# Linear attention and a bilinear feed-forward on one core: a column a chunk for the outputs' scale, the keys' features a slot later, the parts of v spread, and two kinds of hi parts written by ScalarE instead of GpSimd

## The chip, the cores and the metric

The kernel runs on one core of one Trainium2 chip. The metric is the device time of one execution in microseconds (us). Engines are named as in the profile: PE is TensorE (PEld its weight loads), DVE is VectorE, ACT is ScalarE, POOL is GpSimd, SP is SyncE, whose queue issues most of the transfers here.

## What is computed

The reference is a kernelised attention (8 batches, 8 heads, 576 positions, head size 64, 128 features) and then a feed-forward on 4608 tokens of width 512:

```python
def phi(x):
    proj = np.einsum('bhsd,md->bhsm', x, omega)
    sq = np.sum(x * x, axis=-1, keepdims=True) / 2.0
    h = proj - sq
    h = h - np.max(h, axis=-1, keepdims=True)
    return np.exp(h) / np.sqrt(m)
q_p, k_p = (phi(q_s), phi(k_s))
kv = np.einsum('bhsm,bhsd->bhmd', k_p, v)
z = np.sum(k_p, axis=2)
num = np.einsum('bhsm,bhmd->bhsd', q_p, kv)
den = np.einsum('bhsm,bhm->bhs', q_p, z)[..., None] + 1e-06
out = num / den
...
a = x @ w1
b = x @ w2
h = a * b @ w3
return h @ w_out
```

Everything is float32 (the weights arrive as float64), and `w3 @ w_out` is one matrix that the kernel makes first, W.

## The kernel before

**Precision.** Every float32 operand of a large product is held as two float16 parts: a hi part (the value rounded) and a lo part (value minus hi). A product is then three passes on PE: hi by hi, hi by lo, lo by hi (`PASSES`). So each operand costs a hi operation (a scaled copy) and a lo operation (a subtraction) on some engine. `split` (L135 to L148), `in_parts` (L292 to L298) and `gate` (L630 to L632) do it, and strings such as `KS`, `VS`, `EH`, `EL` say for each chunk which engine does which part: in `VS`, `a` is ACT for hi and DVE for lo, `m` is POOL for hi and DVE for lo.

**The work of a chunk.** The 4608 positions are 36 chunks of 128. For a chunk of q or k: load `qraw` or `kraw` (256 KB, SP's queue, two buffers each); sum of squares on ACT (`junk_q`, `junk_k`, L158); a scale from a small PE product and DVE operations (`norm_q_k`, L163 to L178, L232); hi on ACT (L141) and lo on DVE (L144) into `qhl` and `khl`; 24 matmuls into a pair of PSUM banks (`qpj`, `kpj`, L265); the greatest entry (`nm`, DVE, L275); the subtraction (`qe`, `ke`, DVE, L288); the exponential on ACT (L289); hi and lo parts of the features (`eq`, `ek`: casts at L130 on DVE or L132 on ACT, lo at L298, mostly POOL). The features of q are transposed by DMA (`eqT`, L368).

**Batches.** A batch of 576 positions is five chunks, some of them half. Its v is loaded (`vraw`, L309), measured, scaled and split (`vhl`, L143 or L141 and L144; zeros at L332), and `kv_batch` multiplies features of k by v (`kvp`, 120 matmuls, L346; parts `kv`, L355 and L356).

**Attention and feed-forward of a chunk.** `q_attend` (`nu`, 24 matmuls, L381) and DVE's division (`gd`, `gr`, `xs`, L390 to L396), the greatest entry and its power of two (`mx`, `p2p`, `p2r`, `pt`, L403 to L414), hi on ACT (L417) and lo on DVE (L418) into `xhl`, and a DMA transpose into `xT` (L422). Then two gate units a chunk: 48 matmuls (`ab`, L617), the first half's scaled copy on ACT (`asb`, L626), the product on DVE (L627), hi on POOL (L631), lo on POOL (L632) into a block of `arena`. `project_out` (24 matmuls, `o`, L643) multiplies by W, ACT scales the result (L647) by `osc`, a DVE operation at L639, and SP's queue stores it.

**Buffers that matter.** `qpj`, `kpj`, `nu` and `kvp` take turns in two pairs of PSUM banks: the tile after the next can be written only when this one has been read. A `nu` is read by `xs`, a `kvp` by `kv`, a `kpj` by the subtraction `ke`. `osc` is a pool tile with four buffers: the write of the fifth waits until the ACT operation at L647 has read the first.

**Order.** Python code lays the work out in slots, three for a step, and within a slot by a rank: step i brings `q_chunk(i)` (rank 1) and `k_chunk(i + 5)` (rank 2), and `q_attend` some slots later. Each slot runs one unit of a queue of gates and projections, then what is planned, then one part of v's work (`v_unit`); a batch's leftover parts are run just before its `kv_batch`. What a scheduler then makes of it is a fixed order on every engine; each engine runs its instructions strictly in that order.

Of the kernel before, what the change touches and what calls it, by code (L numbers as in the profile page):

```python
# [9 lines left out]
F32 = mybir.dt.float32  # L10
# [5 lines left out]
ALU = mybir.AluOpType  # L16
# [3 lines left out]
P = 128  # L20
# [10 lines left out]

KS = "a"
QS = "a"
VS = "aaaaam"
WS = "a"
EH = "aaaaaadadadada"
EL = "ddddddpdpdpp"
# [13 lines left out]
EAGER = 40  # L51
EARLY = 6
KV_LAG = 5
RAW64_BUFS = 3
O_BUFS = 2
RAW_BUFS = 2
# [10 lines left out]
def tile_favor_attention_then_bilinear_ffn(  # L67
# [19 lines left out]
    nc = tc.nc  # L87
    NCH = qT.shape[0]
# [14 lines left out]
    const = ctx.enter_context(tc.tile_pool(name="const", bufs=1))  # L103
# [9 lines left out]
    def bank_m(name):  # L113
        return ps_m.tile([P, 512], F32, tag="pm", name=name)

    def small(name, n=1, rows=P, dt=F32, bufs=4):
        return sm.tile([rows, n], dt, tag=f"s_{name}", name=name, bufs=bufs)
# [16 lines left out]
    def pick(kinds, i):  # L134
        return kinds[min(i, len(kinds) - 1)]  # L135
# [82 lines left out]
    for i in range(4):  # L218
        t = const.tile([P, 3], F32, name=f"sums_{i}")
# [82 lines left out]
    def k_chunk(c):  # L302
        e = features(c, "k")
        ek[c] = at.tile([P, 2, H, M], F16, tag="ek", name=f"ek_{c}", bufs=EK_BUFS)
        in_parts(ek[c], e, pick(EH, c), pick(EL, c))
# [20 lines left out]
    def v_split(b, n):  # L326
# [9 lines left out]
        x = vraw[c][r0:r1]  # L336
        split(pick(VS, 5 * b + n), hi, lo, x, sv[b][r0:r1])

# [103 lines left out]
    arena = const.tile([P, ARENA, 512], F32, name="arena")  # L442
    raw_at = list(range(0, 4 * RAW64_BUFS, 4))
    mag_at = list(range(4 * RAW64_BUFS, 4 * RAW64_BUFS + 4, 2))
    free = list(range(4 * RAW64_BUFS + 4, ARENA))

# [157 lines left out]
    def gate(c0, n, u):  # L604

        nf, T = 4 // n, n * P
        x = xT[c0 * P // TOK]
        off = c0 * P % TOK
        ab = []
        for m in range(2):  # L610
            ps = bank_m(f"ab_{c0}_{u}_{m}").rearrange("p (f s) -> p f s", f=nf)
            for k in range(nf):
                f = u * nf + k
                i, r = f // (NF // 2), f % (NF // 2)
                mm = [(cc, a, b) for cc in range(NC) for a, b in PASSES]
                for j, (cc, a, b) in enumerate(mm):
                    nc.tensor.matmul(  # L617
                        ps[:, k],
                        w12[m][i][cc][:, a, r * P : (r + 1) * P],
                        x[:, b, cc, off : off + T],  # L620
                        start=j == 0,
                        stop=j == len(mm) - 1,
                    )
            ab.append(ps)
        asb = mo.tile([P, nf, T], F32, tag="asb", name=f"asb_{c0}_{u}", bufs=ASB_BUFS)
        nc.scalar.mul(asb, ab[0], 2.0**-37)  # L626
        nc.vector.tensor_tensor(asb, ab[1], asb, ALU.mult)  # L627
        place = block()
        left[place] = nf * n
        h = arena[:, place].bitcast(F16).rearrange("p (x f s) -> p x f s", x=2, f=nf)  # L630
        nc.gpsimd.tensor_scalar(h[:, 0], asb, 1.0, 1.0, ALU.mult, ALU.mult)  # L631
        nc.gpsimd.tensor_tensor(h[:, 1], asb, h[:, 0], ALU.subtract)  # L632
        for k in range(nf):
            for t in range(n):
                hs[c0 + t, u * nf + k] = h[:, :, k, t * P : (t + 1) * P], place

    def project_out(c):
        sc = small("osc")
        nc.vector.tensor_scalar(sc, pts[c], pts[c], kap, ALU.mult, ALU.mult)  # L639
        ps = bank_m(f"o_{c}")  # L640
        mm = [(f, a, b) for f in range(NF) for a, b in PASSES]
        for i, (f, a, b) in enumerate(mm):
            nc.tensor.matmul(ps, hs[c, f][0][:, a], W[f][:, b], start=i == 0, stop=i == len(mm) - 1)  # L643
        for f in range(NF):
            used(hs[c, f][1])
        o = mo.tile([P, DO], F32, tag="o", name=f"o_{c}", bufs=O_BUFS)
        nc.scalar.mul(o, ps, sc)  # L647
        nc.sync.dma_start(out[c * P : (c + 1) * P, :], o)
# [3 lines left out]
    B_OF_K = {}  # L652
# [3 lines left out]
    v_work = []  # L656
# [7 lines left out]
    def v_unit():  # L664
        if v_work:
            v_work.pop(0)[1]()
# [26 lines left out]
    for ch in ORDER:  # L693
        n = seen.get(ch, 0)
# [23 lines left out]
    def put(slot, rank, fn):  # L718
        plan.setdefault(slot, []).append((rank, len(plan[slot]) if slot in plan else 0, fn))

    behind_by = []

    def ready(c):
        x_turn(c)
# [14 lines left out]
    def step(i):  # L739
        at0 = begin[i]  # L740
        kc = i + LEAD
        keys = [(n, c) for n, c in (("q", i), ("k", kc)) if 0 <= c < NCH]
        state = {}

        def norms():
            state["am"] = norm(keys, i)

        def splits():
            for name, c in keys:
                split_raw(c, name)  # L750
                if c + 2 < NCH:
                    load(srcs[name], c + 2, name)

        put(at0 - 3, 3, norms)
        put(at0 - 2, 6, lambda: scale(keys, state["am"]))
        put(at0 - 1, 8, splits)
        if i >= 0:
            put(at0, 1, lambda: q_chunk(i))
            lag = 2 if i < EARLY else 5
            put(at0 + lag, 7 if i < EARLY else 0, lambda: q_attend(i))  # L760
            put(at0 + lag + 1, 0, lambda: ready(i))
        if kc < NCH:
            put(at0, 2, lambda: k_chunk(kc))
        if kc in B_OF_K:

            def kv():

                while v_work and v_work[0][0] <= B_OF_K[kc]:
                    v_unit()
                kv_batch(B_OF_K[kc])  # L770


            put(at0 + (2 if i < 0 else KV_LAG - 1 if i < EARLY else KV_LAG), 5, kv)
        for b in range(B):
            cs = [c for c, _, _ in chunks_of(b)]
            if cs[1] == kc:
                put(at0, 9, lambda b=b: v_batch(b))
            if cs[0] == kc:
                put(at0 + 2, 10, lambda cs=cs: [v_load(c) for c in cs if c not in vraw])

    for i in range(first, NCH):
        step(i)
# [4 lines left out]
    for t in range(max(plan) + 1):  # L787
        n = min(PER[t] if t < len(PER) else 1, len(ticks))
        weights(n)
        if not ticks and raw_at:  # L790
            for a, w in [(a, 4) for a in raw_at] + [(a, 2) for a in mag_at]:
                free.extend(range(a, a + w))
            raw_at.clear()
        unit(RESERVE if t > EAGER else 0)
        for _, _, fn in sorted(plan.get(t, []), key=lambda x: x[:2]):
            fn()
        v_unit()
    assert not ticks
    while queue:
        unit()  # L800
# [38 lines left out]
```

## Time and profile before

| what | value |
|---|---|
| three timed runs | 904.66, 906.85, 910.05 us (median 906.85) |
| the profiled execution | 904.25 us, its span 902.5 us |
| mean granted PE clock | 0.951 |
| PE busy | 790.9 us, 88% of the span |
| DVE busy | 622.6 us, 69% |
| ACT busy | 421.0 us, 47% |
| POOL busy | 322.2 us, 36% |

In the rows below, times are us from the span's start and the mean of one instruction is in ns. "[2.68 <-DVE xs L396]" behind a row of the timeline says that its engine sat idle for 2.68 us before it and that DVE's `xs` ended the wait. In a row of groups, "busy, mean | idle" stand in that order. In the rows by stretch, the last three numbers are PE's granted clock (1 is full), the DMA share and GB/s.

### The profile page before, as it was taken

The numbers are of one execution on the slowest core, as the hardware profiler recorded it, in microseconds if no ns is written. First come the engines' busy times: TensorE is split into PE (matmuls) and PEld (weight loads), VectorE is DVE, ScalarE is ACT, GpSimd is POOL, SyncE is SP. The second block draws the span as 40 slices with busy tenths as digits, with TensorE's granted clock in tenths as the row PEclk, the third lists the DMA queues.
The fourth block names the chain that finished last, engine by engine and source line by source line (L and its number), as shares of the span: only waits on it lengthen the run. The fifth ranks groups of instructions, "written<-read, shape, count | busy, mean of one in ns | idle before, by whom it ended". The sixth has DMA issues, their size and how long they took to land.

```text
span 902.5 us, 20601 instructions
## 1 busy us (share of the span) xinstructions
PE 790.9 (88%) x8614; PEld 586.0 (65%) x8614; DVE 622.6 (69%) x1116; ACT 421.0 (47%) x748; POOL 322.2 (36%) x327
## 2 busy tenths in 40 slices
PE   1964499578996998999999999899899899999998
PEld 0433254476875876767777776777677677677674
DVE  5879877788779887766867777778667774553210
ACT  3677874877436535444354335543454333221111
POOL 0000003223364465443634643455444543323221
PEclk9985699789999999999999999999999999999999
DMA  8535455332345353333434443344332232333000
GB/s 311 191 120 196 140 153 170 111 73 55 88 107 105 84 130 83 83 84 83 116 83 77 95 111 71 72 94 113 85 93 65 60 71 61 82 60 60 24 25 35
DMA packets 142525, 88.43 MB, mean 98 GB/s; under 512 B 116704, under 2 KB 116832, under 8 KB 142432
## 3 DMA queue, kind: packets, MB, share of 16 engines
q1 hardware_dynamic: 134944, 66.15, 31.0%
q10 hardware_dynamic: 7488, 20.97, 6.9%
q8 instruction: 67, 1.10, 0.5%
q14 instruction: 26, 0.21, 0.1%
HBM read 49.35 MB, written 9.44 MB: 65 GB/s over the span
## 4 chain that ended last, share of the span: by engine, by line
PE 42%; DVE 28%; ACT 13%; DMA 9%; issue 6%; POOL 1%; SPq 0%; DVEq 0%; ACTq 0%; POOLq 0%
PE ab L617 20%; PE o L643 11%; DVE nm L275 5%; DVE qhl L144 4%; DMA qraw<-qT 4%; PE wp L557 4%; DVE vhl L144 3%; ACT ke L289 2%; DVE qe L288 2%; DVE ke L288 2%; DMA kraw<-kT 2%; ACT ek L132 2%; PE kvp L346 2%; DVE asb L627 2%; PE nu L381 1%
## 5 line engine op out<-in xcount | busy, mean ns | idle before, releaser
L617 PE MATMUL ab<-xT,w12b 128*128 128x256 f16 (+1 forms) x3840 | 400.3, 265 | 10.8 <-DMA xT<-xhl 8.5
L617 PEld LDWEIGHTS <-w12b 128*128 128x128 f16 x3840 | 345.1, 99 | 54.3 <-issue 8.8
L643 PE MATMUL o<-Wb,arena 128*128 128x512 f16 x864 | 193.4, 379 | 2.1 <-DVE Wb L144 1.6
L643 PEld LDWEIGHTS <-arena 128*128 128x128 f16 x864 | 84.3, 100 | 96.3 <-issue 2.9
L631 POOL TENSOR_SCALAR arena<-asb 128x512 f16<-128x512 f32 x72 | 57.6, 800 | 249.7 <-DVE asb L627 238.3
L298 POOL TENSOR_TENSOR eq<-qe,eq 128x1024 f16<-128x1024 f32 x34 | 73.9, 2174 | 147.9 <-DVE eq L130 111.1
L289 ACT ACTIVATE qe<-qe,ln_e,es 128x1024 f32<-128x1024 f32 x31 | 38.4, 1239 | 138.0 <-DVE qe L288 138.0
L632 POOL TENSOR_TENSOR arena<-asb,arena 128x512 f16<-128x512 f32 x72 | 91.4, 1270 | 5.9
L627 DVE TENSOR_TENSOR asb<-ab,asb 128x512 f32<-128x512 f32 x72 | 49.4, 686 | 52.7 <-PE ab L617 50.6
L144 DVE SCALAR_TENSOR_TENSOR qhl<-qraw,s,qhl 128x512 f16<-128x512 f32 x36 | 63.8, 1773 | 28.7 <-ACT qhl L141 28.7
L158 ACT ACTIVATE junk_q<-qraw 128x512 bf16<-128x512 f32 x36 | 22.7, 630 | 120.4 <-DMA qraw<-qT 120.3
L298 POOL TENSOR_TENSOR ek<-ke,ek 128x1024 f16<-128x1024 f32 x28 | 60.2, 2149 | 41.4 <-DVE ek L130 39.8
L265 PE MATMUL kpj<-om,khl 64*128 64x128 f16 x864 | 36.9, 237 | 43.4 <-DVE xs L396 12.1
L639 DVE TENSOR_SCALAR osc<-pt,kap 128x1 f32<-128x1 f32 x36 | 9.5, 271 | 84.8 <-ACT o L647 84.6
L265 PEld LDWEIGHTS <-khl 64*128 64x128 f16 x864 | 29.4, 103 | 50.2 <-ACT junk_k L158 16.1
L557 PE MATMUL wp<-w12b 128*128 128x512 f32 x128 | 60.2, 623 | 1.2 <-DVE w12b L485 1.2
L626 ACT ACTIVATE asb<-ab 128x512 f32<-128x512 f32 x72 | 41.8, 580 | 24.4 <-PE ab L617 24.4
L381 PEld LDWEIGHTS <-eqT 128*128 128x128 f16 (+1 forms) x960 | 32.5, 102 | 26.0 <-DMA eqT<-eq 15.3
L647 ACT ACTIVATE o<-o,osc 128x512 f32<-128x512 f32 x36 | 24.2, 673 | 52.2 <-PE o L643 52.2
L381 PE MATMUL nu<-kv,eqT 128*128 128x65 f16 (+1 forms) x960 | 34.7, 196 | 15.0 <-DMA eqT<-eq 14.3
L418 DVE SCALAR_TENSOR_TENSOR xhl<-xs,p2r,xhl 128x512 f16<-128x512 f32 x36 | 28.8, 800 | 26.5 <-ACT xhl L417 26.4
L143 POOL TENSOR_SCALAR vhl<-vraw,s 128x512 f16<-128x512 f32 (+1 forms) x35 | 36.3, 1054 | 29.4 <-DVE mx L409 11.7
(124 smaller groups left out, 1071.1 us busy)
## 6 DMA issues: line engine op xcount, KB each, us to landing
kraw<-kT SPq DMA_DIRECT2D x36, 256.0 KB, 3.0
vraw<-v SPq DMA_DIRECT2D x36, 256.0 KB, 3.0
qraw<-qT SPq DMA_DIRECT2D x36, 256.0 KB, 2.7
out<-o SPq DMA_DIRECT2D x36, 256.0 KB, 2.0
arena<-w3T ACTq DMA_DIRECT2D x8, 1024.0 KB, 5.9
arena<-w ACTq DMA_DIRECT2D x8, 1024.0 KB, 5.6
arena<-wo ACTq DMA_DIRECT2D x4, 1024.0 KB, 5.1
eqT<-eq SPq DMA_TRANSPOSE x72, 3.1
```

Of the source, the lines that this page charges most:

```text
L144: nc.vector.scalar_tensor_tensor(lo, src, s, hi, ALU.mult, ALU.subtract)
L265: nc.tensor.matmul(pg[:, g, i], hl[d, x, i], om[d, y], start=first is None and n == 0, stop=n == len(PASSES) - 1,)
L275: nc.vector.tensor_reduce(nm, pj, AX.X, ALU.max, negate=True)
L289: nc.scalar.activation(e, e, AF.Exp, scale=es, bias=ln_e)
L298: (nc.vector if lo == "d" else nc.gpsimd).tensor_tensor(t[:, 1], e, t[:, 0], ALU.subtract)
L381: nc.tensor.matmul(nu[r0:r1, h // 4, h % 4], t[:, x, place(h), r0:r1], kvs[b][:, y, h], start=n == 0, stop=n == 2,)
L557: nc.tensor.matmul(ps, w[:, j, k * P : (k + 1) * P], guest[:, j], start=j == j0, stop=j == HALF - 1,)
L617: nc.tensor.matmul(ps[:, k], w12[m][i][cc][:, a, r * P : (r + 1) * P], x[:, b, cc, off : off + T], start=j == 0, stop=j == len(mm) - 1,)
L627: nc.vector.tensor_tensor(asb, ab[1], asb, ALU.mult)
L631: nc.gpsimd.tensor_scalar(h[:, 0], asb, 1.0, 1.0, ALU.mult, ALU.mult)
L632: nc.gpsimd.tensor_tensor(h[:, 1], asb, h[:, 0], ALU.subtract)
L643: nc.tensor.matmul(ps, hs[c, f][0][:, a], W[f][:, b], start=i == 0, stop=i == len(mm) - 1)
```

## The change

Five edits:

- `oscs` is one constant tile with a column for each of the 36 chunks, in place of the four rotating `osc` buffers. The operation and its place in the program text stay.
- From step 8 on (`K_LATE`), `k_chunk` is planned one slot later than `q_chunk` of the same step, so another unit of the queue stands between them.
- The work on v gets a due slot, that of its batch's `kv_batch`; each slot runs as many parts of it as are needed to be done in time, at least one.
- `VS`: the hi parts of v are ACT's in all batches (before, ACT's for five parts and POOL's for the other 35).
- The hi part of a gate's output (72 of them) is a copy on ACT, no longer an operation on POOL. Its lo part stays on POOL.

```diff
-VS = "aaaaam"
+VS = "a"
...
+K_LATE = 8
...
-        nc.gpsimd.tensor_scalar(h[:, 0], asb, 1.0, 1.0, ALU.mult, ALU.mult)
+        nc.scalar.copy(h[:, 0], asb)
         nc.gpsimd.tensor_tensor(h[:, 1], asb, h[:, 0], ALU.subtract)
...
+    oscs = const.tile([P, NCH], F32, name="oscs")
+
     def project_out(c):
-        sc = small("osc")
+        sc = oscs[:, c : c + 1]
         nc.vector.tensor_scalar(sc, pts[c], pts[c], kap, ALU.mult, ALU.mult)
...
-            put(at0, 2, lambda: k_chunk(kc))
+            put(at0 + (i >= K_LATE), 2, lambda: k_chunk(kc))
...
-            put(at0 + (2 if i < 0 else KV_LAG - 1 if i < EARLY else KV_LAG), 5, kv)
+            due[B_OF_K[kc]] = at0 + (2 if i < 0 else KV_LAG - 1 if i < EARLY else KV_LAG)
+            put(due[B_OF_K[kc]], 5, kv)
...
-        v_unit()
+
+        n = max([1] + [-(-(k + 1) // max(due[b] - t, 1)) for k, (b, _) in enumerate(v_work)])
+        for _ in range(n):
+            v_unit()
```

Lines of the kernel after are one higher than before from the features on, and four higher from `project_out` on. In names, the first number is the chunk (for a gate, the first chunk of its group and the unit), the last the buffer's.

On PE, from the keys of chunk 15 on, the 24 matmuls of `kpj` move from between the two gate units of a chunk to behind the second; all else there keeps its order, but for the interleaving of the first projection `o_0` with `nu_4`. On DVE, the greatest entry and subtraction of the keys move with them. This is DVE before, from the second-last gate product of group 16 to its last:

```order
L627 TENSOR_TENSOR asb_16_2_7410<-ab_16_2_1_7385,asb_16_2_7410 128x512
L275 TENSOR_REDUCE nm_7451<-qpj_21_7426 128x8
L288 TENSOR_TENSOR qe_21_7453<-qpj_21_7426,nm_7451 128x1024
L275 TENSOR_REDUCE nm_7487<-kpj_26_7462 128x8
L288 TENSOR_TENSOR ke_26_7489<-kpj_26_7462,nm_7487 128x1024
L130 CAST eq_21_7456<-qe_21_7453 128x1024
L627 TENSOR_TENSOR asb_16_3_7554<-ab_16_3_1_7529,asb_16_3_7554 128x512
```

And the same place on DVE after the change:

```order
L628 TENSOR_TENSOR asb_16_2_7396<-ab_16_2_1_7371,asb_16_2_7396 128x512
L276 TENSOR_REDUCE nm_7437<-qpj_21_7412 128x8
L289 TENSOR_TENSOR qe_21_7439<-qpj_21_7412,nm_7437 128x1024
L131 CAST eq_21_7442<-qe_21_7439 128x1024
L628 TENSOR_TENSOR asb_16_3_7507<-ab_16_3_1_7482,asb_16_3_7507 128x512
L276 TENSOR_REDUCE nm_7537<-kpj_26_7512 128x8
L174 TENSOR_SCALAR norm_q22_k27_7545<-norm_q22_k27_7545 128x3
L289 TENSOR_TENSOR ke_26_7539<-kpj_26_7512,nm_7537 128x1024
```

The cast of q's features, which needs ACT's exponential, now follows directly on the subtraction, and the keys come behind the second gate product.

The second place is DVE from the lo part of the keys to the lo part of x, in the same chunk; before:

```order
L144 SCALAR_TENSOR_TENSOR khl_27_7640<-kraw_27_7056,s3_4_7563,khl_27_7640 128x512
L390 TENSOR_SCALAR gd_7627<-nu_20_7602 128x8
L394 RECIPROCAL gr_7629<-gd_7627 128x8
L639 TENSOR_SCALAR osc_8865<-pt_19_7420,kap_111 128x1
L396 TENSOR_TENSOR xs_20_7631<-nu_20_7602,gr_7629 128x512
L403 TENSOR_REDUCE mx_7633<-xs_20_7631 128x1
L409 TENSOR_SCALAR mx_7633<-mx_7633 128x1
L184 TENSOR_SCALAR p2p1_4_7701<-mx_7633 128x1
L187 RECIPROCAL p2r1_4_7703<-p2p1_4_7701 128x1
L414 TENSOR_SCALAR pt_20_7705<-p2p1_4_7701,pv_5784 128x1
L418 SCALAR_TENSOR_TENSOR xhl_20_7707<-xs_20_7631,p2r1_4_7703,xhl_20_7707 128x512
```

After:

```order
L145 SCALAR_TENSOR_TENSOR khl_27_7625<-kraw_27_7043,s3_4_7549,khl_27_7625 128x512
L391 TENSOR_SCALAR gd_7612<-nu_20_7587 128x8
L395 RECIPROCAL gr_7614<-gd_7612 128x8
L397 TENSOR_TENSOR xs_20_7616<-nu_20_7587,gr_7614 128x512
L404 TENSOR_REDUCE mx_7618<-xs_20_7616 128x1
L410 TENSOR_SCALAR mx_7618<-mx_7618 128x1
L185 TENSOR_SCALAR p2p1_4_7686<-mx_7618 128x1
L188 RECIPROCAL p2r1_4_7688<-p2p1_4_7686 128x1
L415 TENSOR_SCALAR pt_20_7690<-p2p1_4_7686,pv_5775 128x1
L643 TENSOR_SCALAR oscs_114<-pt_20_7690,kap_111 128x1
L419 SCALAR_TENSOR_TENSOR xhl_20_7692<-xs_20_7616,p2r1_4_7688,xhl_20_7692 128x512
```

The scale of an output stood ahead of `xs` and was that of chunk 19, for whose buffer the output of chunk 15 had to be scaled first; now it is that of chunk 20, directly behind its input `pt`.

The third place is ACT over one chunk, from the hi part of x to the scaling of an output; before:

```order
L417 ACTIVATE xhl_19_7422<-xs_19_7341,p2r1_4_7418 128x512
L626 ACTIVATE asb_16_2_7410<-ab_16_2_0_7360 128x512
L289 ACTIVATE qe_21_7453<-qe_21_7453,ln_e_82,es_7275 128x1024
L626 ACTIVATE asb_16_3_7554<-ab_16_3_0_7504 128x512
L289 ACTIVATE ke_26_7489<-ke_26_7489,ln_e_82,es_7275 128x1024
L132 CAST ek_26_7492<-ke_26_7489 128x1024
L141 ACTIVATE qhl_22_7635<-qraw_22_7051,s3_4_7563 128x512
L141 ACTIVATE khl_27_7640<-kraw_27_7056,s3_4_7563 128x512
L158 ACTIVATE junk_q24_8190,sums_0_101<-qraw_24_7638 128x512
L647 ACTIVATE o_15_7599<-o_15_7574,osc_7572 128x512
```

After:

```order
L418 ACTIVATE xhl_19_7408<-xs_19_7327,p2r1_4_7404 128x512
L627 ACTIVATE asb_16_2_7396<-ab_16_2_0_7346 128x512
L159 ACTIVATE junk_k28_7735,sums_3_107<-kraw_28_7339 128x512
L632 CAST arena_112<-asb_16_2_7396 128x512
L290 ACTIVATE qe_21_7439<-qe_21_7439,ln_e_82,es_7262 128x1024
L627 ACTIVATE asb_16_3_7507<-ab_16_3_0_7457 128x512
L632 CAST arena_112<-asb_16_3_7507 128x512
L290 ACTIVATE ke_26_7539<-ke_26_7539,ln_e_82,es_7262 128x1024
L142 ACTIVATE qhl_22_7620<-qraw_22_7038,s3_4_7549 128x512
L133 CAST ek_26_7542<-ke_26_7539 128x1024
L142 ACTIVATE khl_27_7625<-kraw_27_7043,s3_4_7549 128x512
L651 ACTIVATE o_15_7584<-o_15_7559,oscs_114 128x512
```

Each gate's hi part (the casts into `arena`) stands on ACT behind a DVE product and ahead of an exponential; the hi part of q has moved ahead of the cast of the keys' features, and the scaling of the output ahead of `junk_q`, which waits for a load.

In the early part, the parts of v of batch 1 stand apart: two of its five lo parts now come on DVE between the division of chunk 2 and the lo part `xhl_2`, and in SP's queue three of the five loads of the next batch's v move behind the loads of q and k. In the later batches the five lo parts stay together in one chunk.

More of the change, by code (lines that the diff above doesn't have):

```diff
@@ L721, in tile_favor_attention_then_bilinear_ffn @@
     behind_by = []
+    due = {}
     def ready(c):
```

## The prediction

> **What bounds the kernel now.** I first cut the span by stage: busy time by stretch, with the columns PE, PEld, DVE, ACT, POOL and then PE's granted clock.
>
> ```profile
> 0.00:215.00 215.00, 144.10 (x1376) 93.02 (x1377) 171.25 (x316) 150.00 (x305) 31.04 (x46) 0.84 0.52 156
> 215.00:300.00 85.00, 75.89 (x1076) 58.72 (x1075) 70.15 (x122) 42.63 (x73) 33.56 (x36) 0.98 0.39 91
> 300.00:750.00 450.00, 422.24 (x4770) 324.69 (x4767) 331.33 (x574) 199.21 (x326) 219.49 (x210) 0.98 0.38 88
> 750.00:903.00 153.00, 148.65 (x1402) 109.59 (x1400) 49.93 (x106) 29.14 (x45) 38.06 (x37) 1.00 0.21 49
> ```
>
> The last stretch is PE alone; its 4.4 us without matmuls are the drain. So whatever PE loses earlier is added to the end, and a gap removed earlier is gained in full. From 300 to 750, where the change works most, PE idles 27.8 us. The groups of that stretch say where.
>
> ```profile
> L265 PE MATMUL kpj<-om,khl 64*128 64x128 f16 x504 | 19.6, 230 | 25.5 <-DVE xs L396 10.9 <-DVE kv L356 9.2 <-ACT junk_k L158 5.3
> L275 DVE TENSOR_REDUCE nm<-qpj 128x8 f32<-128x1024 f32 x22 | 26.7, 1213 | 0.0
> L639 DVE TENSOR_SCALAR osc<-pt,kap 128x1 f32<-128x1 f32 x23 | 6.2, 270 | 56.4 <-ACT o L647 56.4
> L144 DVE SCALAR_TENSOR_TENSOR qhl<-qraw,s,qhl 128x512 f16<-128x512 f32 x23 | 49.9, 2170 | 24.2 <-ACT qhl L141 24.2
> L418 DVE SCALAR_TENSOR_TENSOR xhl<-xs,p2r,xhl 128x512 f16<-128x512 f32 x22 | 18.3, 832 | 16.8 <-ACT xhl L417 16.7
> ```
>
> 25.5 us of the idle time stand before `kpj`, which waits until DVE has emptied its pair of banks (the 5.3 us put down to ACT's `junk_k` are the same wait: in the largest of the three, `xs` ended just before `kpj` began). DVE in turn stands still for 56.4 us before `osc`, 2.6 us a chunk (22 chunks, by the second row), and hardly ever for PE:
>
> ```profile
> DVE asb L627 <- PE ab L617: 4.5, 5, 1.9
> DVE gd L390 <- PE nu L381: 2.7, 4, 1.8
> ```
>
> So in this stage the chain over DVE sets the pace and PE follows. The timeline around one gap shows why.
>
> ```profile
> 444.46 2.44 DVE L144 SCALAR_TENSOR_TENSOR qhl<-qraw,s,qhl 128x512 f16<-128x512 f32 x1 [1.21 <-ACT qhl L141]
> 446.93 0.33 SPq L213 DMA_DIRECT2D qraw<-qT  x1
> 449.66 0.63 ACT L158 ACTIVATE junk_q<-qraw 128x512 bf16<-128x512 f32 x1 [4.62 <-DMA qraw<-qT]
> 450.29 0.67 ACT L647 ACTIVATE o<-o,osc 128x512 f32<-128x512 f32 x1
> 450.99 0.27 DVE L639 TENSOR_SCALAR osc<-pt,kap 128x1 f32<-128x1 f32 x1 [2.76 <-ACT o L647]
> 451.18 0.68 DVE L396 TENSOR_TENSOR xs<-nu,gr 128x512 f32<-128x512 f32 x1
> 452.01 1.47 PE L265 MATMUL kpj<-om,khl 64*128 64x128 f16 x24 [2.68 <-DVE xs L396]
> ```
>
> DVE frees `qraw`, the load takes 2.7 us, ACT sits in front of `junk_q` until it lands, scales the output only then, and DVE cannot write the fifth `osc` before that: a tiny operation ties DVE to a load that DVE itself released.
>
> The gaps cost more than themselves. PE's timeline and the stretches behind the gaps:
>
> ```profile
> 349.25 1.46 PE L265 MATMUL kpj<-om,khl 64*128 64x128 f16 x24 [3.80 <-DVE xs L396]
> 392.80 0.97 PE L265 MATMUL kpj<-om,khl 64*128 64x128 f16 x24 [2.10 <-DVE kv L356]
> ...
> 496.04 1.47 PE L265 MATMUL kpj<-om,khl 64*128 64x128 f16 x24 [2.21 <-DVE kv L356]
> ...
> 579.40 0.85 PE L265 MATMUL kpj<-om,khl 64*128 64x128 f16 x24 [3.26 <-DVE kv L356]
> ...
> 720.16 0.85 PE L265 MATMUL kpj<-om,khl 64*128 64x128 f16 x24 [2.56 <-DVE xs L396]
> ```
>
> ```profile
> 350.00:360.00 10.00, 10.00 (x79) 7.21 (x75) 8.25 (x16) 5.40 (x7) 3.63 (x3) 0.88 0.21 40
> 390.00:400.00 10.00, 7.90 (x92) 6.33 (x89) 8.26 (x9) 4.03 (x6) 2.92 (x3) 0.83 0.14 27
> 450.00:460.00 10.00, 7.99 (x77) 6.72 (x78) 6.78 (x12) 5.94 (x14) 1.77 (x2) 0.83 0.25 67
> 490.00:500.00 10.00, 7.79 (x93) 6.40 (x91) 8.27 (x14) 3.84 (x8) 1.77 (x2) 0.83 0.25 55
> 570.00:580.00 10.00, 6.74 (x98) 5.86 (x96) 5.55 (x15) 5.05 (x12) 1.48 (x12) 1.00 0.40 104
> 720.00:730.00 10.00, 9.84 (x84) 7.37 (x85) 8.90 (x18) 4.43 (x6) 2.72 (x3) 0.83 0.21 53
> ```
>
> After five gaps of 2.1 to 3.8 us the granted clock falls for a while: (1 - 0.83) x 10 = 1.7 us of full-speed work, 1.2 us for the first. That is 8.0 us. After the gap of 3.26 us it does not fall, and in the gapless 750 to 903 it is 1.00.
>
> **The change, part by part.** *The column of scales and the later keys* go together: each alone attacks the same 25.5 us. Without the `osc` wait `xs` comes up to 2.8 us earlier, and with the keys behind the second gate `kpj` needs its banks one unit later. A gate unit is 48 matmuls, 5.2 to 5.4 us at full clock, more than the longest wait, 3.80 us. So both covers would have to fail for the old waits to stay: 25.5 us gone, and with them the 8.0 us of low clock. At the new place, `nu` needs `qpj`'s banks a unit and a projection after `qpj`, and the next `qpj` needs `kpj`'s about 11 us after it: no new wait by the banks. For the keys' lateness their parts have slack, since `kv_batch` uses them chunks later.
>
> On clocks, the Trainium skill ("TensorE: Matmul & The Clock Gate", What's actually happening) says that only an idle window of about 3.4 us makes PE slow. This trace differs: 2.10 us was followed by 0.83. By the page, four of the five drops would not come from the gaps and could stay, and the sum would be 6.8 us higher.
>
> What is late next? The DVE chain. Per chunk it takes 450 / 22 = 20.5 us now, of which osc 2.6. PE's own work is (422.2 - 8.0) / 22 = 18.8 us. The chain without osc is 17.9 us; but q's cast now stands directly behind the subtraction and waits for an exponential on ACT:
>
> ```profile
> L289 ACT ACTIVATE qe<-qe,ln_e,es 128x1024 f32<-128x1024 f32 x22 | 27.3, 1240 | 105.2 <-DVE qe L288 105.2
> L132 ACT CAST ek<-ke 128x1024 f16<-128x1024 f32 x22 | 23.0, 1045 | 0.7
> ```
>
> That adds 1.2 us, 19.1 us in all. Against it, q's hi part no longer stands behind the cast `ek` (1.05 us, most of the 24.2 us of waits above), and the keys' lo part may now meet POOL's `ek` in its place. I take 19.0 us, 0.2 over PE's, so 22 x 0.2 = 5 us stay as new waits, with bounds of 0 and 22 (below).
>
> *Hi parts on ACT.*
>
> ```profile
> L631 POOL TENSOR_SCALAR arena<-asb 128x512 f16<-128x512 f32 x45 | 39.6, 880 | 126.7 <-DVE asb L627 126.7
> L143 POOL TENSOR_SCALAR vhl<-vraw,s 128x512 f16<-128x512 f32 (+1 forms) x25 | 25.0, 1017 | 19.5 <-DVE mx L409 11.7 <-DVE pv L324 7.5
> L141 ACT ACTIVATE vhl<-vraw,s 128x512 f16<-128x512 f32 (+1 forms) x5 | 3.7, 745 | 0.9 <-DVE s L178 0.9
> ```
>
> The first two rows are the stage from 300 to 750, the third the whole span. In the stage POOL loses 45 + 25 operations, 64.6 us, and ACT gains 70 x 0.745 = 52 us: from 199 to 251 us of 450. That is room, since it spends 105.2 us there waiting for `qe` alone. (Over the whole span it is 72 + 35 operations, 80 us for ACT.) What is queued behind a gate's cast is the next exponential; PE needs neither soon. Cost on PE's path: nothing as long as that holds; the price if not is the last rival.
>
> *Parts of v and the early stage.* Before 215 us ACT is busy 150 of 215 and several waits are chains over DVE and ACT, such as
>
> ```profile
> 184.56 7.42 PE L617 MATMUL ab<-xT,w12b 128*128 128x128 f16 x96 [6.31 <-DMA xT<-xhl]
> ...
> 302.57 5.41 PE L617 MATMUL ab<-xT,w12b 128*128 128x256 f16 x48 [2.14 <-DMA xT<-xhl]
> ```
>
> Ahead of the `xhl` that ends the first wait there now stand two lo parts of v, about 0.75 us each undisturbed: +1.5. But DVE has less of v to do at 150 us, and there the moves help by about a microsecond; casts on ACT cost some elsewhere. No row prices all this: +1.5, bounds -2 and +5. Ahead of the second wait `xhl` has moved in front of the keys' subtraction and two exponentials: -2.1, bounds -2.1 and 0. The tail and the drain stay.
>
> **The sum,** against the profiled execution: 904.25 - 25.5 - 8.0 - 2.1 + 1.5 + 5.0 = 875.2 us. That execution is 2.6 us below the median of the three runs (906.85) and below the lowest of them, so for a median I add about 1: **876 us**.
>
> **Rivals.**
>
> *DVE stays the bound.* The lo parts of v fall on one chunk in four or five, and the keys' lo part may be blocked by POOL for most of `ek`. If the chain takes 19.8 us a chunk rather than 19.0, 22 x 1.0 = 22 us of waits take the place of the old ones: 876 + 17 = 893 us. For it: DVE waited for PE only 7.2 us in 450. Against: POOL has 64.6 us less to do in this stage, and `qhl` at 2170 ns against 832 for `xhl`, an operation of the same kind and size, shows what DVE can win back where POOL is out of the way.
>
> *No change.* The waits return elsewhere, before `nu` or `qpj`, because the loads of q are the true pace (2.7 us each, ACT idle 4.62 us for one above). Then all but the start is given back: 902 to 906 us. Against: `junk_q` has slack once nothing but ACT's own queue waits behind it.
>
> *Slower: ACT's queue takes osc's place.* Each gate's cast waits on ACT for DVE's product; behind it wait the exponential, then DVE's cast, then the keys. If the casts stand wholly on the chain, a chunk gains 2 x 0.72 us for them, 1.24 for the exponential and 25 / 22 x 0.745 = 0.85 for v, 3.5 us, against the 2.6 of `osc`: 904.25 + 22 x 0.9 = 924 us. It decides from 2.6 us a chunk on. The Trainium skill ("TensorE: Matmul & The Clock Gate", the table at its head) calls ScalarE's queue a strict FIFO, which this needs; the wait of the output behind `junk_q` above agrees. Against: ACT would have to be the last to arrive each time, and it idles 56% of the stage.
>
> **How the numbers follow.** PE-bound as forecast, 866 to 884: 0.64. DVE-bound, to 894: 0.22. A small gain above that: 0.04. No change within 0.5% (about what a measurement of this kernel can tell): 0.05. Slower: 0.05. The range 866 to 894 holds the first two, 0.86: its low end has all waits gone (871) and the early stage 2 better with a little more from 215 to 300; its high end is the DVE case. Faster by over 0.5%: 0.90.
>
> **What would show it.** Right: no wait of DVE before `oscs`; `kpj`'s waits under 3 us in the steady stage, which ends near 720 instead of 750; a clock of 1.00 there; POOL near 225 us (322 less 107 x 0.92) and ACT near 500. Wrong: PE idle before `qpj`, `nu` or the gates by more than 10 us; ACT idle before its casts while DVE waits for an exponential; gaps gone but the clock still dropping; or a PE idle time before 300 us that grew by more than 5.

## The result and the profile after

The changed kernel takes 876.13 us (median of 4 runs, 874.61 to 877.41) against 907.68 us (4 runs, 904.66 to 910.05) for the kernel before on the same chip: a ratio of 0.9653, 95% interval 0.962 to 0.9687. Its profiled execution took 876.11 us with a span of 874.3 us, 28.2 us shorter than the span before (902.5 us). The forecast was 876 us.

Busy time by engine, from the page of the kernel after:

```profile
PE 786.8 (90%) x8608; PEld 581.6 (67%) x8614; DVE 604.2 (69%) x1116; ACT 481.9 (55%) x855; POOL 221.6 (25%) x220
```

PE was busy 790.9 us before, so 4.1 us of the 28.2 come from less time in matmuls, and 24.1 us from less idle time (111.6 to 87.5 us). Busy time by stretch in the kernel after (columns PE, PEld, DVE, ACT, POOL, then PE's granted clock) shows where the idle time went:

```profile
0.00:300.00 300.00, 216.21 (x2356) 149.10 (x2363) 239.15 (x440) 205.46 (x401) 45.00 (x61) 0.87 0.48 139
300.00:750.00 450.00, 450.00 (x5248) 345.43 (x5247) 329.18 (x605) 246.82 (x410) 154.10 (x143) 1.00 0.40 92
```

From 300 to 750 us PE no longer idles at all; before it idled 27.8 us there. Up to 300 us its idle time grew, from 80.0 to 83.8 us. The groups of the stretch from 300 to 750 us in the kernel after:

```profile
L266 PE MATMUL kpj<-om,khl 64*128 64x128 f16 x504 | 17.7, 217 | 0.0
L643 DVE TENSOR_SCALAR oscs<-pt,kap 128x1 f32<-128x1 f32 x26 | 7.0, 271 | 0.9
L628 DVE TENSOR_TENSOR asb<-ab,asb 128x512 f32<-128x512 f32 x46 | 31.6, 686 | 13.4 <-PE ab L618 13.0 <-ACT asb L627 0.4
L391 DVE TENSOR_SCALAR gd<-nu 128x8 f32<-128x8 f32 x24 | 3.7, 154 | 5.3 <-PE nu L382 5.3
L145 DVE SCALAR_TENSOR_TENSOR qhl<-qraw,s,qhl 128x512 f16<-128x512 f32 x24 | 20.4, 849 | 33.8 <-ACT qhl L142 33.4 <-DMA eqT<-eq 0.4
L145 DVE SCALAR_TENSOR_TENSOR khl<-kraw,s,khl 128x512 f16<-128x512 f32 x21 | 43.6, 2077 | 16.2 <-ACT khl L142 16.2
```

The gaps before `kpj` and DVE's wait before the scale are gone, and the roles have turned round: DVE now waits for PE, 13.0 + 5.3 us, where it waited 4.5 + 2.7 us before. The last two rows show a trade: the lo part of q fell from 2170 to 849 ns, that of k rose from 1164 to 2077 ns. The row of k before:

```profile
L144 DVE SCALAR_TENSOR_TENSOR khl<-kraw,s,khl 128x512 f16<-128x512 f32 x21 | 24.4, 1164 | 0.0
```

What was lost stands in the first 305 us. PE's timeline in the kernel after:

```profile
184.78 7.39 PE L618 MATMUL ab<-xT,w12b 128*128 128x128 f16 x96 [8.22 <-DMA xT<-xhl]
...
276.19 0.39 PE L266 MATMUL qpj<-om,qhl 64*128 64x128 f16 x4 [5.12 <-ACT qhl L142]
...
298.71 4.99 PE L347 MATMUL kvp<-vhl,ek 128*128 128x65 f16 x120 [2.90 <-DVE ke L289]
```

The first wait was 6.31 us before; both kernels still start this gate at the same time (184.56 and 184.78 us), because PE had come there earlier. The last is new: with keys a slot later, the first key-value sum of the new order finds them unfinished. It stands in place of the wait of 2.14 us at 302.57 us.

### The profile page after: what moved, and what is told of

Same layout as the page of the kernel before. It is cut to its first block, busy times and chain, and to the rows that moved or that the text cites. A ratio compares the mean times of both kernels' runs of the same rounds, so it can differ in the third digit from the quotient of the medians.

```text
span 874.3 us, 20591 instructions
## 1 busy us (share of the span) xinstructions
PE 786.8 (90%) x8608; PEld 581.6 (67%) x8614; DVE 604.2 (69%) x1116; ACT 481.9 (55%) x855; POOL 221.6 (25%) x220
## 4 chain that ended last, share of the span: by engine, by line
PE 78%; DVE 9%; ACT 5%; DMA 4%; issue 2%; POOL 1%; SPq 0%; ACTq 0%; DVEq 0%
PE ab L618 40%; PE o L647 20%; PE wp L558 6%; PE kvp L347 3%; PE nu L382 3%; PE qpj L266 3%; PE kpj L266 2%; DVE nm L276 2%; PE wp L556 1%; DMA kraw<-kT 1%; ACT ke L287 1%; DMA arena<-wo 1%; PE norm_q_k L164 1%; DMA eqT<-eq 1%; DVE vhl L145 1%
## 5 line engine op out<-in xcount | busy, mean ns | idle before, releaser
L618 PE MATMUL ab<-xT,w12b 128*128 128x256 f16 (+1 forms) x3840 | 395.1, 263 | 10.4 <-DMA xT<-xhl 8.2
L633 POOL TENSOR_TENSOR arena<-asb,arena 128x512 f16<-128x512 f32 x72 | 84.5, 1174 | 293.6 <-ACT arena L632 292.8
L632 ACT CAST arena<-asb 128x512 f16<-128x512 f32 x72 | 44.4, 616 | 85.3 <-DVE asb L628 85.3
L145 DVE SCALAR_TENSOR_TENSOR khl<-kraw,s,khl 128x512 f16<-128x512 f32 x36 | 56.0, 1557 | 16.2 <-ACT khl L142 16.2
L145 DVE SCALAR_TENSOR_TENSOR qhl<-qraw,s,qhl 128x512 f16<-128x512 f32 x36 | 32.3, 898 | 37.7 <-ACT qhl L142 37.3
L290 ACT ACTIVATE ke<-ke,ln_e,es 128x1024 f32<-128x1024 f32 x27 | 33.5, 1240 | 43.0 <-DVE ke L289 43.0
L418 ACT ACTIVATE xhl<-xs,p2r 128x512 f16<-128x512 f32 x36 | 25.8, 718 | 40.2 <-DVE p2r L188 38.6
L558 PEld LDWEIGHTS wp<-w12b 128*128 128x128 f32 x128 | 25.3, 202 | 32.5 <-issue 29.7
L276 DVE TENSOR_REDUCE nm<-kpj 128x8 f32<-128x1024 f32 x36 | 43.8, 1217 | 3.5 <-PE kpj L266 3.3
```

The lines of the kernel that those rows point to most:

```text
L145: nc.vector.scalar_tensor_tensor(lo, src, s, hi, ALU.mult, ALU.subtract)
L276: nc.vector.tensor_reduce(nm, pj, AX.X, ALU.max, negate=True)
L290: nc.scalar.activation(e, e, AF.Exp, scale=es, bias=ln_e)
L558: nc.tensor.matmul(ps, w[:, j, k * P : (k + 1) * P], guest[:, j], start=j == j0, stop=j == HALF - 1,)
L618: nc.tensor.matmul(ps[:, k], w12[m][i][cc][:, a, r * P : (r + 1) * P], x[:, b, cc, off : off + T], start=j == 0, stop=j == len(mm) - 1,)
L632: nc.scalar.copy(h[:, 0], asb)
```

## The experiments

The runs, each beside the kernel before on its own chip:

| kernel | median us | ratio to before, 95% interval |
|---|---|---|
| column of scales alone | 888.85 | 0.9812 (0.9786 to 0.9838) |
| five buffers for the scale, nothing else | 887.97 | 0.9806 (0.9773 to 0.9838) |
| keys a slot later alone | 876.71 | 0.9683 (0.9658 to 0.9708) |
| hi parts on ACT alone | 897.35 | 0.9907 (0.9881 to 0.9933) |
| all but the later keys | 888.79 | 0.9822 (0.9786 to 0.9857) |
| later keys alone, k split ahead of q | 883.43 | 0.9764 (0.9723 to 0.9805) |
| all, `EH` = a | 871.51 | 0.9636 (0.9593 to 0.9679) |
| all, later keys from step 12 | 873.76 | 0.9659 (0.9622 to 0.9696) |
| all, once more | 874.43 | 0.9643 (0.9622 to 0.9665) |
| all but the hi parts on ACT | 877.88 | 0.9676 (0.9653 to 0.9699) |
| all, `EH` = a and step 12 | 870.96 | 0.9606 (0.9582 to 0.963) |
| all but the spread of v | 875.98 | 0.9668 (0.9635 to 0.97) |

**The column alone.** The kernel before with this edit:

```diff
-        sc = small("osc")
+        sc = oscs[:, c : c + 1]
```

> The kernel before with the column of scales alone: the gate's hi parts stay on GpSimd, v's as they were, k's features in their old slot. Theory of the prediction: DVE's waits at the scale (28 of them, 84.6 us in the profile of before) tie DVE to the arrival of q, and the 25.5 us before the k projections and 8.0 us of lowered clock follow from that alone; without them about 904.25 - 25.5 - 8.0 = 871, with up to half of the new-wait term (5 us) and the 302.57 wait kept, 870 to 882. DVE shows no wait before the scale. Rival 'k's place is the cause': DVE is late at the k projections for other reasons, and PE still reaches them too early: gaps before them of over 15 us remain, 890 to 903. Rival 'GpSimd is the cause': the k lo parts and kv copies still run against GpSimd's gate work, 890 to 907.

888.85 us, some 16 less than before: between the theory's 882 and the rivals' 890, so none of the three has it. DVE's wait at the scale is gone, but PE's timeline of this kernel still has four of the old gaps, all behind `kv`:

```profile
390.56 1.47 PE L265 MATMUL kpj<-om,khl 64*128 64x128 f16 x24 [4.43 <-DVE kv L356]
489.02 1.46 PE L265 MATMUL kpj<-om,khl 64*128 64x128 f16 x24 [2.47 <-DVE kv L356]
569.75 0.85 PE L265 MATMUL kpj<-om,khl 64*128 64x128 f16 x24 [2.81 <-DVE kv L356]
668.42 0.85 PE L265 MATMUL kpj<-om,khl 64*128 64x128 f16 x24 [2.29 <-DVE kv L356]
```

So the 25.5 us before `kpj` were two things: the gaps behind `xs` (16.2 us, with those put down to `junk_k`), which the column clears, and the gaps behind `kv` (9.2 us before, 12.0 us here), which it does not. The timeline ahead of the first shows how `kv` came late:

```profile
383.38 0.63 ACT L158 ACTIVATE junk_q<-qraw 128x512 bf16<-128x512 f32 x1 [4.51 <-DMA qraw<-qT]
...
384.01 0.67 ACT L650 ACTIVATE o<-o,oscs 128x512 f32<-128x512 f32 x1
...
387.00 0.70 ACT L417 ACTIVATE xhl<-xs,p2r 128x512 f16<-128x512 f32 x1
387.61 0.58 ACT L355 ACTIVATE kv<-kvp 128x520 f16<-128x520 f32 x1
387.74 0.75 DVE L418 SCALAR_TENSOR_TENSOR xhl<-xs,p2r,xhl 128x512 f16<-128x512 f32 x1 [3.23 <-ACT xhl L417]
...
389.71 0.70 DVE L356 SCALAR_TENSOR_TENSOR kv<-kvp,kv 128x520 f16<-128x520 f32 x1
```

ACT still stands 4.51 us before `junk_q` for the load of q, and behind it in its queue are not only the output but also `xhl` and `kv`. The scale was one of three ties between the load and DVE; with it cut, DVE waits for `xhl` in its place (45.6 us from 300 to 750, where it was 16.8).

**Five buffers.** The kernel before with one more buffer for the scale:

```diff
-        sc = small("osc")
+        sc = small("osc", bufs=5)
```

> The kernel before with five rotating buffers for the scale in place of four, and nothing else. A scale now waits for the output five chunks back, not four, which ran about 19 us earlier, while the waits are 84.6 / 28 = 3.0 us each. Theory (the wait is only for a free buffer): the waits go to under 5 us in all, and the time is that of the kernel with the column alone within 3 us. Rival (DVE is merely early there, and stops at the next thing that comes late): the waits move to another line, and the time stays within 5 us of before.

887.97 us, within 1 us of the column. DVE's group of the scale, from 300 to 750 us in this kernel:

```profile
L640 DVE TENSOR_SCALAR osc<-pt,kap 128x1 f32<-128x1 f32 x25 | 6.7, 268 | 9.4 <-ACT o L648 9.0
```

From 56.4 to 9.4 us, not under 5 as expected; the rest follows the theory. It was the count of buffers, not where the scales lie: one more would have done what 36 columns do.

**The later keys alone.** The kernel before with this edit:

```diff
-            put(at0, 2, lambda: k_chunk(kc))
+            put(at0 + (i >= K_LATE), 2, lambda: k_chunk(kc))
```

> The kernel before with k's features a slot later alone (from the eighth step). Theory of the prediction (each edit alone attacks the same 25.5 us): DVE still waits about 80 us at the scale, but PE has the next chunk's q products ahead of the k projection and no longer reaches it early: gaps before the k projections under 6 us in 302 to 750, 872 to 885. Rival 'DVE's pace is the bound': DVE as the slower chain delays whatever PE does next, the gaps move to the q projections, numerators or gates with the same sum, 895 to 907.

876.71 us: this one line brings what the whole change brings. From 300 to 750 us PE has no gap in this kernel, but the theory was wrong on the way to it. It let DVE go on waiting at the scale, and DVE does not:

```profile
L641 DVE TENSOR_SCALAR osc<-pt,kap 128x1 f32<-128x1 f32 x25 | 6.5, 260 | 7.8 <-ACT o L649 7.8
```

The timeline of this kernel at the place shown above says why:

```profile
378.30 0.66 ACT L649 ACTIVATE o<-o,osc 128x512 f32<-128x512 f32 x1
...
380.38 0.63 ACT L159 ACTIVATE junk_q<-qraw 128x512 bf16<-128x512 f32 x1 [1.42 <-DMA qraw<-qT]
...
384.94 0.58 ACT L356 ACTIVATE kv<-kvp 128x520 f16<-128x520 f32 x1
385.07 0.84 PE L266 MATMUL qpj<-om,qhl 64*128 64x128 f16 x24
...
385.68 0.70 DVE L357 SCALAR_TENSOR_TENSOR kv<-kvp,kv 128x520 f16<-128x520 f32 x1
...
391.19 0.84 PE L266 MATMUL kpj<-om,khl 64*128 64x128 f16 x24
```

With the keys in another slot, the scheduler lays ACT's queue out anew: the output stands ahead of `junk_q`, and `xhl` ahead of `junk_k`. That order is in all kernels here with the later slot, and in none without it. It cuts the ties that the column leaves: `kv` is through 0.5 us after `qpj` ended, against 4.3 us with the column alone, and ACT's wait for the load is 1.42 us, not 4.51.

**The hi parts alone.** The kernel before with these edits:

```diff
-VS = "aaaaam"
+VS = "a"
...
-        nc.gpsimd.tensor_scalar(h[:, 0], asb, 1.0, 1.0, ALU.mult, ALU.mult)
+        nc.scalar.copy(h[:, 0], asb)
```

> The kernel before with the hi parts of the gate's output and of v on ScalarE alone; four buffers of the scale, k's features in the old slot, v's parts one a slot. Theory of the prediction: GpSimd's busy time falls from 300 to near 225 us, DVE's waits at the scale stay, the gaps before the k projections stay, and ScalarE's queue gets longer by 0.6 us a cast ahead of its exponentials and outputs: within 8 us of before, 900 to 915. Rival 'GpSimd is the cause': most of the gain of the whole change comes from here, 876 to 890.

897.35 us: neither the cause nor nothing. DVE's wait at the scale (52.2 us from 300 to 750) and the gaps before `kpj` (23.1 us) stay, as the theory has it:

```profile
L265 PE MATMUL kpj<-om,khl 64*128 64x128 f16 x504 | 18.2, 220 | 23.1 <-DVE kv L356 9.3 <-ACT junk_k L158 7.8 <-DVE xs L396 5.6
```

The span of its profiled execution (894.67 us, the fastest of its four) is 9.6 us shorter than before, and by the page of the profile all of that is PE's busy time (790.9 to 781.0 us), most of it clock: summed over stretches of 10 us, (1 - clock) x 10 is 3.4 us from 300 us on against 8.5 before, and 32.4 against 35.8 up to there. That is in part the luck of one execution: which of nearly the same gaps cost clock depends on where they fall (last section). The other three runs (897.19 to 898.17 us) have mean clocks of 0.946 to 0.952, no higher than those of the kernel before on that chip (0.943 to 0.953), so where their gain of some 7 us lies isn't shown.

**All but the later keys.** The changed kernel with this edit undone:

```diff
-            put(at0 + (i >= K_LATE), 2, lambda: k_chunk(kc))
+            put(at0, 2, lambda: k_chunk(kc))
```

> The changed kernel with k's features back in q's slot; the column of scales, ScalarE's hi parts and v's spread stay. Theory A (after the first runs): the column clears only the gaps where DVE was held at the scale (16.2 us of 25.5); the four before the k projections that wait for the key-value sum's bank (9.2 us before, 12.0 us with the column alone) come from PE reaching the k projection right behind q's, and only the later slot clears them. So 8 to 14 us of such gaps stay, and with ScalarE's parts the time is 878 to 888, the kernel with the column alone being 888.9. Theory B (the prediction's: every edit attacks the same 25.5 us, the rest was chance): 874 to 878.

888.79 us, just above theory A's range and as with the column alone. From 300 to 750 us in this kernel:

```profile
L265 PE MATMUL kpj<-om,khl 64*128 64x128 f16 x504 | 18.3, 221 | 13.7 <-DVE kv L356 11.6 <-DVE xs L396 2.0
```

The four `kv` gaps are back. Theory B, the prediction's, is out; and the 8 us of the hi parts are not there once the scale is free.

**k ahead of q.** The later keys alone, with the two splits of a chunk swapped:

```diff
-            for name, c in keys:
+            for name, c in keys[::-1]:
                 split_raw(c, name)
```

> The kernel with k's later slot alone, and in each chunk k's parts split ahead of q's on ScalarE and DVE, so that the lo part beside GpSimd's subtraction (2.0 us in place of 0.8) and the other one both stand ahead of the freeing of q's buffer. Theory A (PE arrives at the k projection a slot later, and that cover of some 6 us is the gain): q's load starts some 2 to 3 us later in each chunk and ScalarE waits longer for it, DVE waits at the scale again by over 30 us in all, but PE stays without gaps over 1 us in the steady stage, 874 to 882. Theory B (the gain is that q's lo part no longer lies beside GpSimd's subtraction, 2.2 to 0.8 us a chunk, which frees q's buffer earlier): most of the gain is lost, 890 to 905.

883.43 us, just above A's range and far below B's. The collision with GpSimd is back on q and costs PE 2 us of waits in the steady stage; PE and DVE groups from 300 to 750 us in this kernel:

```profile
L618 PE MATMUL ab<-xT,w12b 128*128 128x256 f16 x2208 | 250.5, 274 | 4.2 <-DMA xT<-xhl 4.2
L266 PE MATMUL qpj<-om,qhl 64*128 64x128 f16 x552 | 20.3, 217 | 2.0 <-DVE qhl L145 1.8
L266 PE MATMUL kpj<-om,khl 64*128 64x128 f16 x504 | 17.7, 217 | 0.0
...
L145 DVE SCALAR_TENSOR_TENSOR qhl<-qraw,s,qhl 128x512 f16<-128x512 f32 x24 | 47.0, 1957 | 19.0 <-ACT qhl L142 19.0
L641 DVE TENSOR_SCALAR osc<-pt,kap 128x1 f32<-128x1 f32 x23 | 6.0, 259 | 3.8 <-ACT o L649 3.8
```

The one large wait, 4.2 us, is at 305 us, at the change of the order, and 3.4 us at half clock follow it. So the faster lo part of q is not the gain; what this kernel loses against the later keys alone (7 us) has mostly been lost by the end of that half clock. A's own step failed as well: it let DVE wait over 30 us at the scale, and DVE waits 3.8, since the output again stands ahead of `junk_q`.

**More of k's hi parts on ACT; the later slot from step 12.** Each edit on the changed kernel, by itself:

```diff
-EH = "aaaaaadadadada"
+EH = "a"
```

```diff
-K_LATE = 8
+K_LATE = 12
```

> The changed kernel with the hi part of k's features always by ScalarE (some were DVE's). Aim: the wait of 5.12 us before the q projection at 276 us, where DVE's cast of one took 2.04 us ahead of the scales. Theory A (that cast is on the way to the wait): 1 to 3 us less, 873 to 876. Theory B (other things are as late): within 1.5 us of the changed kernel. In the steady stage, where PE has no gaps, it changes nothing unless ScalarE, then some 8 us busier, becomes late.

> The changed kernel with k's later slot from the twelfth step, not the eighth. Theory A: the wait of 2.90 us before the key-value sum at 298.7 us comes from k's features being a slot later there, and goes (a wait of about 2 us for the transposed rows at 302.6, as before, takes its place); the steps 8 to 11 get back their old gap at the k projection of about 3.8 us at 349: within 3 us of the changed kernel, rather slower, 875 to 880.

871.51 and 873.76 us, both below the ranges given (873 to 876, 875 to 880). With `EH` = a the wait at 276 us, now at 270, falls as theory A has it:

```profile
152.80 0.38 PE L510 MATMUL l<-wab,ones_bf 128*128 128x512 bf16 x1 [0.18 <-ACT wab L506]
...
270.01 0.39 PE L266 MATMUL qpj<-om,qhl 64*128 64x128 f16 x4 [3.58 <-ACT qhl L142]
```

The row at 152.80 us stands at 157.67 us in the changed kernel: most of the gain comes earlier than I expected it, at the first of the casts that move (128 us); behind it a wait of 3.36 us of PE at 136.71 us for a scale on DVE is gone, and with it the half clock from 137.53 to 140.95 us, which the other profiled execution of the changed kernel (below) doesn't have at that place either. With step 12 the wait at 298.71 us is gone, the one of 2.28 us before the gate at 300.44 us is back, and the gap that I expected at 349 us does not come; the difference of 2.4 us is little more than the runs spread, and measured against the kernel before on each chip there is none (0.9659 against 0.9653 and 0.9643).

**Three on one chip.** The changed kernel as it is, the same without the hi parts on ACT (the edits above undone), and with both of the last two edits:

> The changed kernel once more, beside the two that follow, so that differences of a few us are read on one chip. 873 to 878, and no gap over 1 us before PE's matmuls from 305 us on.

> The changed kernel with the hi parts of the gate's output and of v back where they were (on GpSimd; the first of v on ScalarE); the column, the later slot and v's spread stay. Theory A (with the later slot PE has no gaps in the steady stage, so nothing that relieves DVE or GpSimd there can shorten it): within 3 us of the changed kernel, GpSimd busy near 306 us, ScalarE near 420; the wait at 184 us for the transposed rows falls from 8.2 to near 7 us or less. Theory B (ScalarE's parts are worth the 8 us that they brought alone): 880 to 886.

> The changed kernel with the hi part of k's features always by ScalarE and the later slot from the twelfth step. If both single trials add up (4.6 and 2.4 us below the changed kernel's 876.13): 868 to 871. If both only repeat one gain, or the second one's was chance: 870 to 873. The waits left in the profile from 150 us on would be those at 163, 180, 270 and 295 us; none in the steady stage.

874.43, 877.88 and 870.96 us, five runs each. The hi parts are worth 3.5 us beside the rest, above the 3 of theory A and far from the 8 of theory B; the runs of the two overlap (873.89 to 877.11, 876.21 to 879.77), so the size is rough. In neither kernel does PE idle after 305 us, so what they bring lies before. These two profiles put it into PE's busy time (781.6 against 786.1 us), but the first profile of the changed kernel has 786.8 us, so that difference is the clock of an execution and not the hi parts. What recurs is the stretch from the gate that begins at 184.8 us in the changed kernel to the one at 251.9 us: 66.7 to 67.3 us in the eight profiles with the hi parts on ACT, 68.3 to 69.2 us in five with them on GpSimd (72.8 in the sixth, with k ahead of q). That is some 1.5 us; where the rest lies isn't shown. The kernel with both edits is faster than the changed one: its runs (870.21 to 872.87) lie wholly below those of the other (873.89 to 877.11), 3.5 us between the medians. That is less than 4.6 + 2.4 (both taken between chips): the two don't add up, and it is not shown that step 12 adds anything to `EH`.

**All but the spread of v.** The changed kernel with one part of v a slot:

```diff
-        n = max([1] + [-(-(k + 1) // max(due[b] - t, 1)) for k, (b, _) in enumerate(v_work)])
+        n = 1
```

> The changed kernel with v's parts one a slot as before, those left over all at the key-value sum; the rest as changed. Theory A (v's parts lie beside PE's work in the steady stage): 872 to 878, no gap in the steady stage over 1 us. Theory B (parts in a heap hold up DVE's lo parts ahead of the key-value sums, four of them): the gaps there come back in part, 878 to 885.

875.98 us, as theory A has it: the spread changes nothing that can be measured.

## Why the prediction was right, and where it was not

The time came out as forecast, and the bound, the stage and the sign did too. By steps:

- **PE bounds the tail, so a gap is gained in full.** Right for the tail: from the gate matmul that ends the steady stage (754.96 us before, 726.89 us after) to the last one, both kernels take 127.88 us. That the span fell by 28.2 us, about the 27.8 us of idle time, is chance. The same matmuls of the steady stage, before and after:

```profile
339.28:754.96 415.68, 390.23 (x4519) 300.91 (x4516) 298.42 (x518) 183.69 (x301) 197.16 (x183) 0.98 0.37 86
340.52:726.89 386.37, 386.37 (x4519) 296.00 (x4516) 285.77 (x519) 216.81 (x362) 133.00 (x120) 1.00 0.40 91
```

  They take 29.3 us less: 25.5 us of idle time and 8.0 us of lowered clock (five stretches of 3.41 us at half clock, in which PE was busy for 15.95 us) went, and the work itself grew by 4.1 us (390.2 - 8.0 = 382.2 to 386.4). Up to 340 us the kernel after is 1.2 us behind.
- **-25.5 us before `kpj`.** Right in size. The reasoning, "each alone attacks the same 25.5 us", was wrong for the column: alone it gives some 16 us in time and leaves 12.0 us behind `kv`. The step that failed read the rows `xs` 10.9 and `kv` 9.2 as one wait with one cause. They were one wait by the banks, but `kv` comes through ACT's queue, behind `junk_q`, and not through the scale.
- **The later keys as a cover of one gate unit.** The cover was hardly needed. In the kernel after, the banks were empty before PE came even to the old place. At the key-value sum shown above, in this kernel:

```profile
385.28 0.70 DVE L357 SCALAR_TENSOR_TENSOR kv<-kvp,kv 128x520 f16<-128x520 f32 x1
386.27 0.84 PE L266 MATMUL qpj<-om,qhl 64*128 64x128 f16 x24
392.39 0.79 PE L266 MATMUL kpj<-om,khl 64*128 64x128 f16 x22
```

  `kv` ended at 385.98 us and `qpj` at 387.11; so it is at all 20 chunks from 340 to 715 us, by 0.5 us or more. With the later keys alone the banks came after the end of `qpj` at 9 of 20 chunks, 4.9 us in all; the same sum is 23.9 us in the kernel before. This suggests that most of what the later slot brought came from ACT's new order, at most some 5 us of waits from PE's later arrival. That is read from traces; a kernel with the one and without the other wasn't run, so how the gain divides stays an inference. The prediction's text before it shows ACT's new order, and the prediction made nothing of it.
- **-8.0 us of lowered clock.** Right: the sum of (1 - clock) x 10 us from 300 us on fell from 8.5 to 0.7 us, so the drops went with the gaps, and the sum that was 6.8 us higher is refuted here. That there were five drops to win was in part luck: with nearly the same gaps the kernel with the hi parts alone lost 3.4 us there.
- **+5.0 us of new waits.** As waits, 0. The mis-sized term is PE's own work: the q projections of the kernel after stand 19.2 us apart ((712.0 - 346.7) / 19) with PE always busy, against the 18.8 us that I took from 22 chunks in 450 us (there were 450 / 20.7 = 21.7, which makes 19.1). So the DVE chain of 19.0 us was not the longer one, as its 18.3 us of waits for PE show. The rest is the new order, which costs PE time: the two chunks behind the gate at 303 us, without a gap and at full clock in both, with the column alone and in the kernel after:

```profile
302.54:338.95 36.41, 36.41 (x391) 27.98 (x392) 31.39 (x56) 16.08 (x26) 22.38 (x27) 1.00 0.57 117
303.53:340.52 36.99, 36.99 (x396) 27.98 (x393) 29.11 (x55) 19.80 (x32) 13.12 (x19) 1.00 0.45 115
```

  So 4.1 us of longer work stand where the sum had 5.0 us of waits; that the sizes agree is luck.
- **-2.1 us at 302.57 us.** The wait went, and the new one of 2.90 us before `kvp` took its place: +0.8 net. It comes with the later slot (2.6 us with that alone), and the step "their parts have slack, since `kv_batch` uses them chunks later" is what failed, at the one place where the order changes.
- **+1.5 us in the early stage.** The two lo parts ahead of `xhl` are there (8.22 us for 6.31), and PE comes to that place earlier; the net by 185 us is 0.2. From there to the gate at 252 us the kernel after gains 1.6 us. Worse was the clock around the waits at 276 and 298 us. The kernel after from 270 to 310 us:

```profile
270.00:280.00 10.00, 4.88 (x57) 3.11 (x55) 8.57 (x22) 3.50 (x5) 4.24 (x2) 0.70 0.45 105
290.00:300.00 10.00, 7.10 (x107) 6.42 (x102) 7.90 (x17) 6.67 (x13) 3.52 (x3) 0.90 0.52 85
300.00:310.00 10.00, 10.00 (x176) 9.13 (x174) 8.97 (x20) 6.23 (x13) 5.68 (x13) 0.93 0.50 109
```

  That is (0.30 + 0.10 + 0.07) x 10 = 4.7 us, against 1.3 us in the same rows before (0.87, 1.00, 1.00): 3.4 us more, of which 2.0 fell on time in which PE was busy; the sum did not have them.

Up to 340 us the kernel after is 1.2 us slower, where the sum had it 0.6 faster (-2.1 + 1.5); the steady stage is 29.3 us faster, where the sum had 28.5 (25.5 + 8.0 - 5.0). The two errors go against each other (875.2 summed, 876.11 measured), and the second is small only because PE's longer work took the place of the waits: the total is better than its parts.

The rivals: DVE did not stay the bound, ACT's queue did not take the scale's place (a cast into `arena` is 615 ns, not the 745 I took, and PE waits for none of it from 305 us on), and the waits did not move to `nu` or `qpj`. POOL came to 221.6 us (225 worked out), ACT to 481.9 (near 500 worked out, with the dearer cast).

## What to carry to other kernels

When an engine waits at a tiny operation, look at everything else that stands behind the same late instruction in the queue of the engine that it waits for: freeing one of them moves the wait to the next (here from the scale to x's hi part and the key-value sum). A change of a slot also changes the fixed order on engines that it doesn't speak of; read the new order of the engine that waits for loads first. And once the bounding engine has no gaps in a stage, taking waits away wins nothing more there: the last 3.5 us came from the start. A new order can also cost the bounding engine time of its own, here 0.2 to 0.3 us a chunk.

## What the runs showed of the hardware

- PE's clock drops to half for 3.4 us at a time; in the steady stage of the kernel before each drop costs 1.7 us. In every trace the stretches at half clock begin and end on one grid of 3.41 us, whose place differs from execution to execution. From 220 us on, in all fourteen traces, each stretch of this grid at full clock in which PE idled 1.85 us or more was followed by one at half clock (37 in all), and none in which it idled 1.81 us or less was; earlier the limit is less sharp (1.63 us were once enough, and 1.89 us once were not). So the length of a gap alone does not decide. Stretches of the grid, by the same columns (PE's busy time first, its clock third from the end), in the kernel before, around its gaps of 2.10 and 3.26 us:

```profile
389.97:393.38 3.41, 1.31 (x46) 1.16 (x44) 3.10 (x5) 0.94 (x2) 0.04 (x1) 1.00 0.40 77
393.38:396.79 3.41, 3.41 (x25) 2.34 (x20) 3.31 (x3) 1.04 (x1) 1.74 (x2) 0.50 0.00 0
574.29:577.71 3.42, 1.85 (x34) 1.38 (x32) 2.33 (x8) 3.08 (x7) 0.00 (x0) 1.00 0.20 77
577.71:581.12 3.41, 1.72 (x33) 1.55 (x34) 3.27 (x5) 0.00 (x0) 1.10 (x2) 1.00 0.43 82
581.12:584.53 3.41, 3.41 (x33) 3.06 (x32) 3.31 (x3) 1.72 (x2) 0.68 (x1) 1.00 0.00 0
```

  The shorter gap lies in one stretch, which idles 2.10 us; the longer is cut in two, 1.57 and 1.69 us, and costs no clock. In the kernel with the hi parts alone the gap of 2.29 us at 492.05 us is cut as well (1.81 us) and costs none, where its twin before (2.21 us, 1.95 of it in one stretch) did. From 310 us on no kernel without gaps shows a drop. The Trainium skill ("TensorE: Matmul & The Clock Gate", What's actually happening) tells of a free-running window of about 3.4 us and a halved clock: half of 3.4 is the 1.7 measured, and the grid agrees. That the window must be wholly idle, as I read it, these gaps do not bear out: somewhat over half was enough.
- A lo part on DVE (128x512) takes 0.75 us by itself and on the mean 2.0 to 2.2 beside GpSimd's subtraction of k's features (128x1024, 2.13 us); which of q and k pays is a matter of the slot (q 849, k 2077 ns after; q 2170, k 1164 before). A cast on DVE (128x1024) is 0.69 us by itself and took 2.04 us at 272.84 us of the kernel after, beside GpSimd's subtraction of q's features. The Trainium skill ("SBUF — State Buffer", Who interferes with whom) says that a DVE instruction with two SBUF inputs contends with GpSimd's reads, and that casts can; these durations agree.
